# Grouped-head attention beside a GELU MLP, float32: the MLP's first bank in a pool of its own, `hh` products ahead of `hl` in one block, and a different order and shape of the first loads

## The chip, the cores and the metric

The kernel runs on one core of a Trainium2 chip. The metric is the device time of one execution in microseconds. PE is TensorE (its weight load is PEld), DVE is VectorE, ACT is ScalarE, POOL is GpSimd, and SP is SyncE, which here only issues DMAs.

## The reference

x has 2048 tokens of 448 features. Two branches read the same normalised tokens and are added to x.

```python
def _A_ref(x, wq, wk, wv, wo):        # 16 heads of 28, one key and value head for all
    q = (x @ wq).reshape(B, S, H, Dh).transpose(0, 2, 1, 3)
    k, v = x @ wk, x @ wv
    p = _softmax(jnp.einsum("bhqd,bkd->bhqk", q, k) * Dh ** -0.5)
    o = jnp.einsum("bhqk,bkd->bhqd", p, v)
    return o.transpose(0, 2, 1, 3).reshape(B, S, H * Dh) @ wo

def _B_ref(x, w1, b1, w2, b2):
    y = _layernorm(x)
    h = _gelu(jnp.einsum("bsd,df->bsf", y, w1) + b1)   # 1792 wide
    return jnp.einsum("bsf,fd->bsd", h, w2) + b2

xn = _layernorm(x)
return x + _A_ref(xn, wq, wk, wv, wo) + _B_ref(xn, w1, b1, w2, b2)
```

## The kernel before, in words

Tokens are cut into 16 tiles of 128, and these into 4 chunks of 512. Products that need full precision are made of rounded parts: a high part (`xh`, `wah`, `w1h`, `w2h`, `hh`) and the rest (`xl`, `wal`, `w1l`, `w2l`, `hl`), and a product is high times high, high times low and low times high, added up in a PSUM bank. The order on each engine is that of the code (`manual_schedule`); the pools and semaphores decide only what an instruction waits for.

There are three stages.

1. **Projections** (`norm_first`, then the loop over chunks with `q_slot`). For a tile, DVE takes the statistics (`bn`, line 208), `bn_end` makes the mean and the reciprocal deviation out of them (ACT's square root at line 193, then DVE's lines 196 to 199 and the shift at line 242), `center` normalises on ACT (line 284) and writes a doubled last part on DVE or POOL (line 288), and `turn` transposes on PE (line 299), copies the high part out on ACT (line 300) and the low part on DVE (line 303). `norm_first` does that for chunk 0 in two halves of two tiles, with idle products (`spin`, line 432) on PE between. `q_slot` makes 128 columns of q, k, v for a chunk in a bank `qp`; its `evac` copies the bank out on ACT (line 393) and DVE (lines 392 and 400), and SP stores the parts to DRAM (`qd`) and into `ks`. In the meantime `w1_split` and `split_a` cut the weights into parts on ACT and POOL.
2. **MLP** (`mlp1`, `mlp2`). For a chunk c and each of 14 slices ft of 128 hidden units, `mlp1` makes the first layer in a bank of the ring `s0` to `s3` (`spare`, 11 products), and ACT, DVE and POOL make the GELU and its parts `hh` and `hl` of it. `mlp2` follows two slices later and adds 12 products to four banks `m2`, one for each token tile. In the first chunk `w2_split` cuts w2 on ACT (line 376) and DVE (line 377) between them.
3. **Attention** with scores, exponentials on ACT, weighted sums of v, and the output product.

PSUM has 8 banks. In the projections the pools `qpp` (4 banks) and `mp` (3 banks) hold seven of them. When they close (`ph1a.close()`), the pool of the ring `ra` (4 banks) and that of `m2` (4 banks) are laid over them, and the first product into a bank waits until its former content has been read. In the same way the tiles `w2h` and `w2l` lie in SBUF where the tiles of the projections lay, `qe` among them, which SP's stores read; ACT's first `w2h` therefore waits for all eight DMA lanes.

A lane is one of eight semaphores that DMAs take in turn, those of SP's and of ACT's queue together. A DMA that gets a lane whose former DMA has not landed waits for it at its issue, and all behind it on that queue wait too. The loads at the start stand in this order: x's tiles 0, 1, and 2 and 3 together (SP), wv and wk (ACT), wq (SP), x's tiles 4 to 7, b1, b2 (`b2b`), tiles 8 to 11, then slices of w1 and the other tiles of x. `load_rows` loads the last 64 of the 448 rows of a weight twice, into both halves of the partitions, with a DMA for each. `b2b` is first read by POOL at line 636, in the 12th block of the MLP.

Of the kernel before, what the change touches and what calls it, by code (L numbers as in the profile page):

```python
# [10 lines left out]
F32 = mybir.dt.float32  # L11
# [5 lines left out]
PSUM = bass.MemoryType.PSUM  # L17

P = 128
S, D, H, DH, F = 2048, 448, 16, 28, 1792  # L20
NT = S // P
CT = 4
# [17 lines left out]
def block_kernel(ctx, tc, x, wq, wk, wv, wo, w1, b1, w2, b2, out):  # L40
    nc = tc.nc
    pe, act, dve, pool = nc.tensor, nc.scalar, nc.vector, nc.gpsimd
# [3 lines left out]
        return t.bitcast(F32)  # L46

    keep = ctx.enter_context(tc.tile_pool(name="keep", bufs=1))
    dram = ctx.enter_context(tc.tile_pool(name="dram", bufs=1, space=bass.MemoryType.DRAM))
    xt_p = ctx.enter_context(tc.tile_pool(name="xt", bufs=len(KEPT)))  # L50
    xl_p = ctx.enter_context(tc.tile_pool(name="xl", bufs=len(KEPT)))
# [23 lines left out]
    b2b = wp.tile([P, D], F32, name="b2b")  # L75
# [17 lines left out]

    def load_rows(dst, src, cols, q=nc.sync):
        q.dma_start(dst[:, 0:3, :], src[0:384, cols].rearrange("(b p) n -> p b n", p=P))
        q.dma_start(dst[0:64, 3, :], src[384:448, cols])
        q.dma_start(dst[64:128, 3, :], src[384:448, cols])

    def load_x(t0, n):
        if t0 < 2 * CT:  # L100
            c, k = divmod(t0, CT)
            dst = first_raws[c][:, k:k + n, :]
            nc.sync.dma_start(dst, xv[:, t0:t0 + n, :])
            return
        for t in range(t0, t0 + n):
            nc.sync.dma_start(xin[t], xv[:, t, :])
# [11 lines left out]
    wal = wqp.tile([P, 3, CW], F32R, name="wal")  # L118
    kvraw = wqp.tile([P, 4, 2, DH], F32, name="kvraw")
    load_rows(kvraw[:, :, 0, :], wv, slice(0, DH), nc.scalar)  # L120
    load_rows(kvraw[:, :, 1, :], wk, slice(0, DH), nc.scalar)
    def pair():
        return wqp.tile([P, 4, D], F32, name="pair", bufs=1)

    qraw = pair()
    load_rows(qraw, wq, slice(0, D))
    load_x(CT, CT)
    make_identity(nc, ident)
# [10 lines left out]
    pool.memset(f(qm), 0.0)  # L139
    b1r = wqp.tile([NF, P], F32, name="b1r", bufs=1)  # L140
    nc.sync.dma_start(b1r, b1.rearrange("(a p) -> a p", p=P))
    nc.sync.dma_start(b2b, b2[None, :].to_broadcast([P, D]))
    load_x(2 * CT, CT)

    def split_a(src, at):
# [58 lines left out]
    def bn(t):  # L204
        c = t // CT
        if t % CT == 0:
            sts[c] = tmp.tile([P, CT, 6], F32, name="st", bufs=2)
        dve.bn_stats(sts[c][:, t % CT, :], xin[t])

    def bn_end(c, k0=0, n=CT):  # L210
        for k in range(k0, k0 + n):
            dve.bn_aggr(lnp[:, CT * c + k, :], sts[c][:, k, :])
        ts = slice(CT * c + k0, CT * c + k0 + n)
        norms = (False, True) if c else (False,)
        r = rstd(lnrq[:, 0:len(norms), ts], lnp[:, ts, 1], n, norms)
        at = next(r)
        yield
        next(r)
        shift(c in KEPT, ts)
        yield  # L220
        if c in KEPT:
            ratio = ratios[c] = tmp.tile([P, CT], F32, name="ratio", bufs=3)
            dve.tensor_mul(ratio, at[:, 1], lnq[:, ts])
            dve.tensor_mul(ratio, ratio, lnr[:, ts])
        elif c:
            shift(True, ts)
        yield
# [41 lines left out]
    def norm_parts(c, second, first=False, bank=mtile):  # L269
        again, second = second, second or c in KEPT  # L270
        xh = xt_p.tile([P, 4, CW], F32R, name="xh")
        xl = xl_p.tile([P, 4, CW], F32R, name="xl")
        xts[c, second and c not in KEPT] = xh, xl
        xns = {}

        def center(k):
            t = CT * c + k
            if first:
                xn = f(wqp.tile([P, 2, CW], F32R, name="qe", bufs=5))[:, 0, :]
            else:  # L280
                xn = (wqp if k % 2 and not again else tmp).tile([P, 4 * P], F32, name="xn", bufs=1)
            scale, bias = (lnq, lnqb) if second else (lnr, lnb)
            src = lines.pop(t) if again else xin[t]
            act.activation(xn[:, 0:D], src, AF.Identity, bias=bias[:, t:t + 1], scale=scale[:, t:t + 1])
            xns[k] = xn

            def doubled():
                (pool if 0 < c else dve).tensor_scalar(
                    xn[:, D:512], src[:, 384:448], scale[:, t:t + 1], bias[:, t:t + 1], op0=ALU.mult, op1=ALU.add)

            if first and k == 1:
                return doubled
            doubled()

        def turn(k, lows=None):
            sl = slice(k * P, (k + 1) * P)
            pt = bank([P, 4, P])
            for b in range(4):
                pe.transpose(pt[:, b, :], xns[k][:, b * P:(b + 1) * P], ident)
            act.activation(xh[:, :, sl], pt, AF.Copy)  # L300

            def low():
                dve.tensor_sub(xl[:, :, sl], pt, f(xh[:, :, sl]))

            low() if lows is None else lows.append(low)

        return center, turn

    def norm_first(bank):
        center, turn = norm_parts(0, False, True, bank)  # L310
        ends = [bn_end(0, 0, 2), bn_end(0, 2, 2)]
        lows = []
        bn(0)
        bn(1)
        next(ends[0])
        next(ends[0])
        center(0)
        bn(2)
        bn(3)
        doubled = center(1)  # L320
        next(ends[1])
        doubled()
        next(ends[1])
        spin(16)
        turn(0, lows)
        spin(3)
        turn(1, lows)
        center(2)
        center(3)
        for low in lows:  # L330
            low()
        spin(6)
        turn(2)
        spin(1)
        turn(3)
        next(first)
# [13 lines left out]
    def w1_load(s):  # L350
        raw = rawtile([P, 4, HD])
        load_rows(raw, w1, slice(s * HD, (s + 1) * HD))
        wl_q.append(raw)

    def w1_load2(s):
        raw = pair()
        load_rows(raw, w1, slice(s * HD, (s + 2) * HD))
        wl_q.extend((raw[:, :, 0:HD], raw[:, :, HD:D]))
# [64 lines left out]
    load_x(3 * CT, CT)  # L423
    w1_load(1)
    w1_load2(2)

    def qbank(shape):
        return qpp.tile(shape, F32, name="qp")

    def spin(n, t=None):  # L430
        for _ in range(n):
            pe.matmul(idle if t is None else t, ident, ident, start=True, stop=True)

    idle = mtile([P, P])
    norm_first(qbank)
    g = stats(1)
    later_one = lambda g=g: next(g)
# [29 lines left out]
    for c in range(NCH):  # L467
        if c + 1 < NCH:
            center, turn = norm_parts(c + 1, False, bank=lambda shape: (qbank, mtile)[next(turns) % 2](shape))
        for i in range(4):  # L470
# [24 lines left out]
            if i in ((1, 3), (1, 2), (1, 3), (0, 2))[c]:  # L495
                n = 2 * c + (i - 1 if c == 1 else i // 2 if c == 3 else i // 3)
# [57 lines left out]
    ring_a = ctx.enter_context(tc.tile_pool(name="ra", bufs=1, space=PSUM))  # L554

    turn_a = itertools.count()

    def spare(shape=(P, CW)):
        return ring_a.tile(list(shape), F32, name=f"s{next(turn_a) % 4}")

    ph1b = ExitStack()
    hp = ph1b.enter_context(tc.tile_pool(name="hp", bufs=3))
# [24 lines left out]
    def mlp2(c, ft, then=None):  # L587
        if ft == 0:
            m2s[c] = [m2p.tile([P, CW], F32, name=f"m2_{k}")[:, 0:D] for k in range(CT)]
        m2 = m2s[c]  # L590
        hh, hl = hs.pop((c, ft))
        terms = ((hh, w2h), (hh, w2l), (hl, w2h))
        for k in range(CT):
            for i, (h, w) in enumerate(terms):
                pe.matmul(m2[k], h[:, k * P:(k + 1) * P], w[:, ft, :], start=(ft == 0 and i == 0),  # L595
                          stop=(ft == NF - 1 and i == 2))
            if ft == NF - 1:
                t = CT * MLP_ORDER[c] + k
                a = lines.pop(t)
                dve.tensor_add(a, a, m2[k])  # L600
                nc.sync.dma_start(ad[:, t, :], a)
            if then is not None:
                then()

    early = []
# [4 lines left out]
    def score_bank():  # L610
        n = next(turn_s) % 7 if ring_b else 0
        return ring_b[0].tile([P, CW], F32, name=f"t{n - 4}") if n > 3 else spare()
# [10 lines left out]
    for c in range(len(KEPT), NCH):  # L623
        g = norm_gen(MLP_ORDER[c], spare)
        for i in range(2 * CT + 1):
            norms[NF * (c - 1) + 4 + i] = lambda g=g: next(g, None)
    for n in range(len(mslots) + 2):
        c, ft = mslots[n] if n < len(mslots) else (NCH, n - len(mslots))
        if 3 <= ft < 11 and ft % 2 and len(KEPT) <= c + 1 < NCH:
            line(CT * MLP_ORDER[c + 1] + (ft - 3) // 2)  # L630
        k = ft - (10 if c < NCH - 1 else 5)
# [21 lines left out]
        if n >= len(mslots):  # L653
            t = f(xl_p.tile([P, 4, CW], F32R, name="xl"))
            early.extend(t[:, k, :] for k in range(4))
            mlp2(*mslots[n - 2], then=lambda: scores(*todo.pop(0)))
        elif n >= 2:
            mlp2(*mslots[n - 2])
# [216 lines left out]
```

## Time and profile before

| | us |
|---|---|
| median of 3 runs (899.61 to 900.98) | 900.62 |
| the profiled execution's own time | 901.05 |
| its span | 899.2 |
| PE busy in it | 883.6 |

A row of the timeline gives the start in us from the span's start, the duration, the engine, the line, what is written and read, and in brackets the idle time ahead of it with what ended it. Where instructions of one kind follow each other, they are merged into a row with their count. A row of waits gives the waiting engine and line, what it waited for, the sum, the number and the longest. The stages are easy to find in the timeline: the first transpose on PE is at 8.04 us, the first MLP product at 66.08 us, and the last second-layer product ends at 353 us.

### The profile page before, as it was taken

What the parts mean: (1) busy time and instruction counts of PE and PEld (TensorE: products, weight loads), DVE (VectorE), ACT (ScalarE), POOL (GpSimd) and SP (SyncE); (2) the same over time, 40 slices, a digit from 0 to 9 for tenths busy, and PEclk for the clock granted to TensorE, in tenths of its full rate; (3) what the DMA queues carried; (4) which work ended last, traced back from release to release, by engine and by line L of the source; (5) the groups of instructions that cost most, each with busy time, mean ns of one, the idle gap of its engine ahead of it and who ended that gap; (6) DMA issues with size and microseconds to landing.
All of it is one profiled execution on the core that took longest, in us unless ns stands there. A gap on an engine that the chain in (4) does not pass through costs nothing.

```text
span 899.2 us, 13110 instructions
## 1 busy us (share of the span) xinstructions
PE 883.6 (98%) x4925; PEld 572.8 (64%) x4925; DVE 313.3 (35%) x584; ACT 670.8 (75%) x1285; POOL 156.4 (17%) x149
## 2 busy tenths in 40 slices
PE   8989999999999999999999999999999999999996
PEld 7867888888888887444554554554555555555552
DVE  7865445344445343222132132132132132232223
ACT  5764444333444346999999999999999999999993
POOL 6443343233235342000000000000000000000000
PEclk9999999999999999999999999999999999999999
DMA  9692112002001402412013021013031113031001
GB/s 294 197 277 68 42 62 82 1 0 83 11 24 41 90 11 78 104 41 52 13 41 93 11 83 52 20 33 93 11 86 49 30 28 89 12 93 42 1 1 44
DMA packets 35022, 55.86 MB, mean 62 GB/s; under 512 B 5694, under 2 KB 21644, under 8 KB 34956
## 3 DMA queue, kind: packets, MB, share of 16 engines
q1 hardware_dynamic: 33548, 54.42, 21.6%
q8 instruction: 40, 0.66, 0.3%
q10 hardware_dynamic: 1408, 0.57, 0.2%
q14 instruction: 26, 0.21, 0.1%
HBM read 39.23 MB, written 14.68 MB: 60 GB/s over the span
## 4 chain that ended last, share of the span: by engine, by line
PE 91%; DVE 3%; ACT 2%; DMA 2%; issue 1%; SPq 0%; POOL 0%; ACTq 0%; DVEq 0%; POOLq 0%
PE po L727 26%; PE s L616 17%; PE m L595 14%; PE t L616 12%; PE s L175 12%; PE s L180 1%; PE s L178 1%; PE qp L175 1%; PE s L694 1%; PE s L695 1%; PE s L696 1%; DMA qd<-qe 1%; PE t L694 1%; PE t L695 1%; PE t L696 1%
## 5 line engine op out<-in xcount | busy, mean ns | idle before, releaser
L618 ACT ACTIVATE p<-s 128x512 f32<-128x512 f32 x582 | 316.9, 679 | 16.1 <-PE s L616 16.0
L618 ACT ACTIVATE p<-t 128x512 f32<-128x512 f32 x434 | 243.9, 680 | 11.0 <-PE t L616 11.0
L727 PE MATMUL po<-p,vs 128*32 128x512 f32 x2032 | 237.7, 597 | 0.0
L616 PE MATMUL s<-xh,ks 128*128 128x512 f32 x590 | 180.3, 406 | 0.0
L616 PEld LDWEIGHTS s<-xh,ks 128*128 128x128 f32 x590 | 107.6, 188 | 65.3 <-ACT p L618 23.4
L616 PE MATMUL t<-xh,ks 128*128 128x512 f32 x434 | 136.9, 406 | 0.0
L727 PEld LDWEIGHTS po<-p,vs 128*32 128x32 f32 x2032 | 56.3, 109 | 123.9 <-issue 118.5
L576 ACT ACTIVATE hx<-s,b1t 128x512 f32<-128x512 f32 x56 | 38.5, 687 | 115.4 <-PE s L180 105.7
L616 PEld LDWEIGHTS t<-xh,ks 128*128 128x128 f32 x434 | 79.3, 188 | 49.0 <-ACT p L618 18.3
L584 POOL TENSOR_TENSOR hl<-hx,hh 128x512 fp32r<-128x512 f32 x56 | 77.6, 1386 | 184.8 <-DVE hh L583 175.7
L718 POOL TENSOR_TENSOR otl<-oc,oth 128x512 fp32r<-128x512 f32 x15 | 19.4, 1295 | 488.7 <-DVE oth L717 450.8
L595 PE MATMUL m<-w2l,hh 128*128 128x448 f32 x224 | 82.6, 369 | 0.9 <-DVE w2l L377 0.9
L595 PE MATMUL m<-w2h,hh 128*128 128x448 f32 x224 | 82.4, 368 | 0.5 <-DVE a L600 0.4
L595 PE MATMUL m<-w2h,hl 128*128 128x448 f32 x224 | 82.0, 366 | 0.7 <-POOL hl L584 0.7
L578 DVE SCALAR_TENSOR_TENSOR hz<-hz,hx 128x512 f32<-128x512 f32 x56 | 45.4, 811 | 106.1 <-ACT hz L577 106.0
L579 ACT ACTIVATE hz<-hz 128x512 f32<-128x512 f32 x56 | 35.4, 632 | 49.9 <-DVE hz L578 49.9
L175 PE MATMUL s<-xh,w1h 128*128 128x512 f32 x168 | 66.4, 395 | 2.4 <-DVE qe L400 2.4
L698 DVE TENSOR_TENSOR row<-row,s 128x448 f32<-128x448 f32 x33 | 20.5, 622 | 133.6 <-PE s L696 133.6
L175 PE MATMUL s<-xl,w1h 128*128 128x512 f32 x168 | 66.4, 395 | 0.0
L175 PE MATMUL s<-xh,w1l 128*128 128x512 f32 x168 | 66.2, 394 | 0.0
L698 DVE TENSOR_TENSOR row<-row,t 128x448 f32<-128x448 f32 x27 | 16.8, 622 | 115.3 <-PE t L696 115.3
L580 DVE SCALAR_TENSOR_TENSOR hx<-hz,hx 128x512 f32<-128x512 f32 x56 | 39.1, 699 | 43.3 <-ACT hz L579 43.3
(174 smaller groups left out, 925.2 us busy)
## 6 DMA issues: line engine op xcount, KB each, us to landing
xh<-qd SPq DMA_DIRECT2D x64, 224.0 KB
qd<-qe SPq DMA_DIRECT2D x24, 256.0 KB
a<-in_A_x_dram SPq DMA_DIRECT2D x24, 224.0 KB
ad<-a SPq DMA_DIRECT2D x16, 224.0 KB
qm<-qd SPq DMA_DIRECT2D x64, 56.0 KB
row<-ad SPq DMA_DIRECT2D x16, 224.0 KB
raw<-in_B_w_dram SPq DMA_DIRECT2D x7, 448.0 KB
out_dram<-row SPq DMA_DIRECT2D x14, 224.0 KB
```

Of the source, the lines that this page charges most:

```text
L175: pe.matmul(ps, w, v, start=(n == 0), stop=False)
L576: act.activation(hx, ph, AF.Identity, bias=b1t[:, ft:ft + 1])
L578: dve.scalar_tensor_tensor(hz, hz, 1.0, hx, op0=ALU.add, op1=ALU.mult)
L579: act.activation(hz, hz, AF.Tanh, scale=GELU[1])
L580: dve.scalar_tensor_tensor(hx, hz, 1.0, hx, op0=ALU.add, op1=ALU.mult)
L584: pool.tensor_sub(hl, hx, f(hh))
L595: pe.matmul(m2[k], h[:, k * P:(k + 1) * P], w[:, ft, :], start=(ft == 0 and i == 0), stop=(ft == NF - 1 and i == 2))
L616: pe.matmul(s, ks[:, kt * P:(kt + 1) * P], qss[u][:, j, :], start=True, stop=True)
L618: act.activation(p, s, AF.Exp, scale=SCALE)
L698: dve.tensor_add(a, a, po)
L718: pool.tensor_sub(otl, oc, f(oth))
L727: pe.matmul(pos[u][32 * j:32 * j + 32, :], vs[:, kt, :], ps[u, kt, j], start=(kt == 0), stop=(kt == NT - 1))
```

## The change

1. A pool `r0` with one bank is opened at the very start, and `s0` of the ring comes from it; `s1` to `s3` stay in `ra`, which has three banks now.
2. In the very first block of the second layer (c = 0, ft = 0), the `hh` products of all four token tiles come first, then those of `hl`.
3. `load_rows` loads the doubled last rows with one DMA that reads its source twice.
4. `b2b` is loaded after the first slices of w1 instead of ahead of x's tiles 8 to 11.
5. In `norm_first`, `bn(2)` comes between the two steps of `bn_end` for tiles 0 and 1, ahead of the reciprocal.

```diff
     keep = ctx.enter_context(tc.tile_pool(name="keep", bufs=1))
+    ring_0 = ctx.enter_context(tc.tile_pool(name="r0", bufs=1, space=PSUM))
...
     def load_rows(dst, src, cols, q=nc.sync):
         q.dma_start(dst[:, 0:3, :], src[0:384, cols].rearrange("(b p) n -> p b n", p=P))
-        q.dma_start(dst[0:64, 3, :], src[384:448, cols])
-        q.dma_start(dst[64:128, 3, :], src[384:448, cols])
+        load_last(dst, src, cols, q)
+
+    def load_last(dst, src, cols, q=nc.sync):
+        q.dma_start(dst[:, 3, :], src[384:448, cols][None].to_broadcast([2, 64, dst.shape[-1]]))
...
     nc.sync.dma_start(b1r, b1.rearrange("(a p) -> a p", p=P))
-    nc.sync.dma_start(b2b, b2[None, :].to_broadcast([P, D]))
     load_x(2 * CT, CT)
...
         next(ends[0])
+        bn(2)
         next(ends[0])
         center(0)
-        bn(2)
         bn(3)
         doubled = center(1)
...
     w1_load2(2)
+    nc.sync.dma_start(b2b, b2[None, :].to_broadcast([P, D]))
...
     def spare(shape=(P, CW)):
-        return ring_a.tile(list(shape), F32, name=f"s{next(turn_a) % 4}")
+        n = next(turn_a) % 4
+        return (ring_a if n else ring_0).tile(list(shape), F32, name=f"s{n}")
...
         terms = ((hh, w2h), (hh, w2l), (hl, w2h))
+        early = c == 0 and ft == 0
+        if early:
+            for k in range(CT):
+                for i, (h, w) in enumerate(terms[:2]):
+                    pe.matmul(m2[k], h[:, k * P:(k + 1) * P], w[:, ft, :], start=(i == 0), stop=False)
         for k in range(CT):
             for i, (h, w) in enumerate(terms):
+                if early and i < 2:
+                    continue
```

Three places in the order of the instructions. The first is on DVE, in `norm_first`: `st` holds a tile's statistics, `rs` the terms of the reciprocal deviation, `lnrq` and `lnb` its scale and shift, `qe` the centred tile. Before:

```order
L208 BN_STATS st<-rows 128x6 x2
L212 BN_AGGR lnp<-st 128x2 x2
L194 TENSOR_SCALAR rs_193<-lnp 128x2
L196 RECIPROCAL rs_193<-rs_193 128x2
L197 SCALAR_TENSOR_TENSOR rs_193<-rs_193 128x2
L198 TENSOR_TENSOR rs_193<-rs_193 128x2
L199 SCALAR_TENSOR_TENSOR lnrq<-rs_193 128x2
L242 SCALAR_TENSOR_TENSOR lnb<-lnp,lnrq 128x2
L288 TENSOR_SCALAR qe<-rows,lnrq,lnb 128x64
L208 BN_STATS st<-rows 128x6 x2
```

The same place of the changed kernel:

```order
L210 BN_STATS st<-rows 128x6 x2
L214 BN_AGGR lnp<-st 128x2 x2
L196 TENSOR_SCALAR rs_190<-lnp 128x2
L210 BN_STATS st<-rows 128x6
L198 RECIPROCAL rs_190<-rs_190 128x2
L199 SCALAR_TENSOR_TENSOR rs_190<-rs_190 128x2
L200 TENSOR_TENSOR rs_190<-rs_190 128x2
L201 SCALAR_TENSOR_TENSOR lnrq<-rs_190 128x2
L244 SCALAR_TENSOR_TENSOR lnb<-lnp,lnrq 128x2
L290 TENSOR_SCALAR qe<-rows,lnrq,lnb 128x64
L210 BN_STATS st<-rows 128x6
```

The third tile's statistics have moved ahead of the reciprocal of the first two tiles.

The second place is on PE, where the MLP begins: `qp` is the last bank of the projections, `s_...` a bank of the ring, and the brackets hold the semaphores for which an instruction waits. Before:

```order
L178 MATMUL qp<-xh,wah 128x512
L180 MATMUL qp<-xl,wah 128x512
L175 MATMUL s_926<-xh,w1h 128x512 [waits DVE_49,PE_49]
L175 MATMUL s_926<-xl,w1h 128x512
L175 MATMUL s_926<-xh,w1l 128x512
```

The same place of the changed kernel, with the end of the first bank and the start of the second:

```order
L180 MATMUL qp<-xh,wah 128x512
L182 MATMUL qp<-xl,wah 128x512
L177 MATMUL s_920<-xh,w1h 128x512
...
L182 MATMUL s_920<-xl,w1h 128x512
L177 MATMUL s_947<-xh,w1h 128x512 [waits DVE_49,PE_49]
```

The wait for the projections' banks has moved from the first bank of the ring to the second, 11 products later.

The third place is on PE, in the first block of the second layer: `m_0` to `m_3` are the four banks. Before:

```order
L595 MATMUL m_0_999<-w2l,hh 128x448 [waits DVE_49]
L595 MATMUL m_0_999<-w2h,hl 128x448 [waits Pool_49]
L595 MATMUL m_1_1000<-w2h,hh 128x448
L595 MATMUL m_1_1000<-w2l,hh 128x448
L595 MATMUL m_1_1000<-w2h,hl 128x448
```

The same place of the changed kernel:

```order
L601 MATMUL m_0_993<-w2l,hh 128x448 [waits DVE_49]
L601 MATMUL m_1_994<-w2h,hh 128x448
L601 MATMUL m_1_994<-w2l,hh 128x448
L601 MATMUL m_2_995<-w2h,hh 128x448
L601 MATMUL m_2_995<-w2l,hh 128x448
L601 MATMUL m_3_996<-w2h,hh 128x448
L601 MATMUL m_3_996<-w2l,hh 128x448
L606 MATMUL m_0_993<-w2h,hl 128x448 [waits Pool_49]
L606 MATMUL m_1_994<-w2h,hl 128x448
```

The wait for POOL's `hl` stood at the third product of the block and stands at the ninth now; that for DVE's `w2l` is at the second, as it was.

## The prediction

> **What bounds the kernel now.** I read the page's busy times first, then the list of waits with PE as the waiting engine.
>
> ```profile
> PE 883.6 (98%) x4925; PEld 572.8 (64%) x4925; DVE 313.3 (35%) x584; ACT 670.8 (75%) x1285; POOL 156.4 (17%) x149
> ```
>
> ```profile
> PE s L175 <- DVE qe L400: 2.4, 1, 2.4
> PE qp L299 <- ACT qe L284: 1.3, 1, 1.3
> PE m L595 <- DVE w2l L377: 0.9, 2, 0.7
> ```
>
> TensorE (PE) works 98% of the span, so a microsecond counts only where PE waits or runs slowly. The longest wait is a single one of 2.4 us, at the MLP's first product (line 175, tile `s`), until DVE has finished line 400. The diff bears on all three. PE's timeline around the first, and the same stretch cut into windows (PE, PEld, DVE, ACT, POOL busy; granted clock, DMA share, GB/s):
>
> ```profile
> 63.25 0.39 PE L180 MATMUL qp<-xl,wah 128*128 128x512 f32 x1
> 66.08 0.77 PE L175 MATMUL s<-xh,w1h 128*128 128x512 f32 x1 [2.44 <-DVE qe L400]
> ...
> 70.24 0.39 PE L175 MATMUL s<-xh,w1h 128*128 128x512 f32 x1
> ...
> 72.75 0.39 PE L175 MATMUL s<-xh,w1h 128*128 128x512 f32 x1
> ```
>
> ```profile
> 63.00:66.05 3.05, 0.64 (x3) 0.19 (x2) 2.82 (x5) 1.63 (x3) 2.27 (x2) 1.00 0.87 263
> 66.05:69.50 3.45, 3.42 (x8) 2.80 (x9) 0.00 (x0) 0.00 (x0) 0.00 (x0) 0.51 0.89 320
> 69.50:72.00 2.50, 2.50 (x12) 2.05 (x12) 0.26 (x1) 1.27 (x2) 0.00 (x0) 1.00 0.03 10
> ```
>
> The wait costs more than its own length. After it the clock is granted at 0.51 for about 3.4 us, in which PE gets through 8 products. The first group of 11 takes 70.24 - 66.08 = 4.16 us, the second 72.75 - 70.24 = 2.51 us: another 1.65 us is lost to the clock.
>
> **The first bank.** Bank `s0` now has a pool of its own, and PE's order shows its first product without a wait; the wait for DVE stands at the second bank's first product. The projections' last product starts at 63.25 and the pace is 2.51/11 = 0.23 us, so the first group runs from 63.48 to 65.99. The second bank is released when the first was, at 66.08. So the second group starts at 66.08 where it started at 70.24: **-4.16 us** (2.51 of it the gap, 1.65 the clock). What is left at the second bank is 0.1 us of waiting; each further 0.1 us by which the release slips costs 0.1 us. The first group's other inputs were split and in use long before.
>
> The Trainium skill, "TensorE: Matmul & The Clock Gate", in its part on the HAM clock gate, says that PE falls to half rate after at least one idle window of about 3.4 us, in windows that run freely. By that rule a 2.44 us gap would not slow the clock, and the first term would be 2.51 us instead of 4.16 us. The window rows differ from it: half clock follows this gap at once.
>
> **The order of the first second-layer products.** ACT, DVE, POOL and PE there, each from its own timeline:
>
> ```profile
> 73.01 0.94 ACT L376 ACTIVATE w2h<-raw 128x896 fp32r<-128x896 f32 x1
> ```
>
> ```profile
> 73.86 0.43 DVE L583 CAST hh<-hx 128x512 fp32r<-128x512 f32 x1
> 74.26 1.09 DVE L377 SCALAR_TENSOR_TENSOR w2l<-raw,w2h 128x896 fp32r<-128x896 f32 x1
> ```
>
> ```profile
> 74.43 2.05 POOL L584 TENSOR_TENSOR hl<-hx,hh 128x512 fp32r<-128x512 f32 x1 [8.57 <-DVE hh L583]
> ```
>
> ```profile
> 75.24 0.36 PE L595 MATMUL m<-w2h,hh 128*128 128x448 f32 x1
> 76.54 0.47 PE L595 MATMUL m<-w2h,hl 128*128 128x448 f32 x1 [0.67 <-POOL hl L584]
> ...
> 78.67 0.39 PE L175 MATMUL s<-xh,w1h 128*128 128x512 f32 x1
> ...
> 81.19 0.36 PE L595 MATMUL m<-w2h,hh 128*128 128x448 f32 x1
> ...
> 83.63 0.39 PE L175 MATMUL s<-xh,w1h 128*128 128x512 f32 x1
> ```
>
> The first block of 12 takes 78.67 - 75.24 = 3.43 us, the next 83.63 - 81.19 = 2.44 us: 0.99 us is lost, most of it waiting for POOL's `hl`. With eight `hh` products ahead (8 x 0.2 = 1.6 us), `hl` is asked for 7.0 us after the second group's start, and POOL had it after 76.48 - 70.24 = 6.24 us, so that wait goes. What is late next is `w2l`, in the second product. ACT's `w2h` ran 2.77 us after the second group's start (73.01 - 70.24), but it waits for every DMA lane, because its tile lies in memory that the projections' stores still read:
>
> ```profile
> 62.27 4.92 SPq L409 DMA_DIRECT2D qd<-qe  x8
> ```
>
> SP issues the last stores until 67.19, and the windows show the transfers busy (0.89) until 69.5, then 0.03. Before, that was over in time. Now 69.5 is 3.4 us after the second group's start: `w2h` runs 0.65 us later in the chain, and `w2l` ends at 3.4 + 0.94 + 1.09 = 5.4 us, where PE wants it at 5.2 us (75.24 - 70.24 + 0.2); with the handovers I take 0.4 us of waiting. So the block loses 0.4 instead of 1.0 us: **-0.6 us**. Bounds: -1.0 us (stores drain sooner, as SP has fewer issues behind it) and 0 (the drain ends 0.6 us later). The other `w2l` wait, at the third block, hangs on a chain that moves along with PE; I leave it at nothing. In blocks after the first the sequence is as before.
>
> **The start.** DVE, ACT, PE and POOL, from the timeline of the first 30 us:
>
> ```profile
> 3.78 0.63 DVE L208 BATCH_NORM_STATS2 st<-rows 128x6 f32<-128x448 f32 x1 [3.78 <-DMA rows<-in_A_x_dram]
> 4.50 1.28 ACT L420 ACT_TABLE_LOAD   x1 [4.50 <-DMA kvraw<-in_A_wv_dram]
> 4.60 0.63 DVE L208 BATCH_NORM_STATS2 st<-rows 128x6 f32<-128x448 f32 x1 [0.19 <-DMA rows<-in_A_x_dram]
> 5.47 0.17 DVE L194 TENSOR_SCALAR rs<-lnp 128x2 f32<-128x2 f32 x1
> 5.91 0.28 ACT L193 ACTIVATE rs<-lnp,one 128x2 f32<-128x2 f32 x1
> 6.22 0.17 DVE L196 RECIPROCAL rs<-rs 128x2 f32<-128x2 f32 x1 [0.57 <-ACT rs L193]
> 7.22 1.41 ACT L284 ACTIVATE qe<-rows,lnb,lnrq 128x448 f32<-128x448 f32 x2 [1.04 <-DVE lnb L242]
> 7.46 1.14 DVE L208 BATCH_NORM_STATS2 st<-rows 128x6 f32<-128x448 f32 x2
> 8.04 0.66 PE L299 MATMUL qp<-ident,qe 128*128 128x128 f32 x4 [1.27 <-ACT qe L284]
> 10.54 0.41 POOL L158 TENSOR_SCALAR wah<-pair 128x256 fp32r<-128x256 f32 x1 [0.61 <-DMA pair<-in_A_wq_dram]
> 11.71 0.32 POOL L160 TENSOR_TENSOR wah<-pair,wah 64x64 fp32r<-64x64 f32 x1
> 11.85 0.60 PE L299 MATMUL qp<-ident,qe 128*128 128x128 f32 x4
> 17.18 0.19 PEld L178 LDWEIGHTS qp<-xh,wah 128*128 128x128 f32 x1 [0.21 <-POOL wah L153]
> ```
>
> PE runs nearly without a gap from 8.04 to 63.64, so what sets 8.04 moves all that follows: reciprocal, scale and shift, ACT line 284, first transpose. The reciprocal waited for ACT until 6.22, and ACT was late (table load at 4.50) because its last key/value load had waited for a DMA lane. The change merges loads, so ACT is free sooner. But `bn(2)` now stands ahead of the reciprocal on DVE, and it needs the third load of x (tokens' tiles 2 and 3, 448 KB). The first two, 224 KB each, had landed by 3.78 and 4.60, 0.82 us apart; at that rate 448 KB land 1.64 us later, at 6.24. Then bn(2) takes half of 1.14 us, and the reciprocal starts at about 6.83 instead of 6.22: **+0.61 us**. Queued behind it on DVE are that whole chain and, through ACT, PE's transposes; PE's idle stretch there grows from 1.27 to 1.9 us. Bounds: if the load is in by 5.64 (5.47 + 0.17), bn(2) runs beside ACT's square root and costs nothing; a gain is excluded because bn(2) alone reaches 6.2. At the other end the load had landed by 7.46, since DVE ran bn(2) then without a wait: reciprocal at 8.06, +1.84 us. I take 6.24, the value of the nearest rows.
>
> SP's own waits show what held wq's load (line 95) at its issue:
>
> ```profile
> SPq L95 <- DMA rows<-in_A_x_dram: 1.6, 1, 1.6
> ```
>
> Now it has a lane at once. It lands no later than before, and POOL's splits finish no later, while PE comes 0.61 us later: the 0.21 us wait at 17.18 goes, **-0.21 us**. More cannot be had: ahead of the first projection PE's transposes end last (11.85 + 0.60 = 12.45), after POOL's first split (11.71 + 0.32 = 12.03).
>
> **Cost nothing.** The merged 64-row loads move the same bytes; they take seven issues off SP and two off ACT's queue, and none of PE's waits names a store or a later load. Moving `b2b` on SP past fourteen loads (x's tiles 8 to 15 and the first slices of w1) takes its 224 KB out of their way; POOL first reads it some ten MLP blocks of 5 us (2.51 + 2.44) after 66 us, so its landing is covered many times over. SP's first `ks` stores now have four issues fewer ahead of them. Should a merged load land late, DVE's or POOL's splits would be late by as much, and PE has the 0.6 us by which it comes later itself as cover.
>
> **The sum.** The profiled execution took 901.05 us, its span 899.2. 901.05 - 4.16 - 0.60 + 0.61 - 0.21 = 896.7 us. It stands 0.43 us above the median of the runs (900.62) and beyond the highest (900.98); I take off half of that: **896.5 us**.
>
> **Rivals.**
> - *The slow clock appears elsewhere.* PE's idle stretch at the start grows to 1.9 us, on the way to the 2.44 us that was followed by half clock; 1.27 us was not. Then 1.65 us come back: 896.5 + 1.65 = 898.2. Chance 0.12.
> - *The slow stretch was not the gap's.* If it comes by its own timing and stays, the first term is 2.51 us: 898.2. The windows speak against it (0.51 exactly from the gap's end). It is the result by the Trainium skill's clock-gate rule above, which the trace does not bear out. Chance 0.10.
> - *The third load lands at 7.46.* Reciprocal 1.23 us later than I take it: 897.7. Chance 0.09.
> - *The change does not do what it says*, and the first group still waits out the last evacuation. Only the other terms are left: 900.8 - 0.2 = 900.6. PE's order speaks against it. Chance 0.04.
> - *Slower.* wq's 672 KB, issued 1.6 us sooner, share the transfer engines with the third load of x, and bn(2) holds the whole chain. Place: DVE ahead of the reciprocal. If the load lands only with wq, near 10.4 (POOL saw wq at 10.54), the reciprocal starts at 11.0, 4.8 us late; PE idles long enough for slow clock, +1.65. 901.05 - 4.76 - 0.21 + 4.8 + 1.65 = 902.5. It decides from a landing at about 8.9 on. Against it: wq is issued behind that load on the same queue. The Trainium skill, "DMA: Bandwidth & Descriptors", under queues, rings and completion order, states that each DMA engine consumes the descriptors of one queue in order; by it this rival falls away. No run here shows yet how these two loads share. Chance 0.03.
>
> **How the numbers follow.** The forecast as worked has the other 0.62. Its own ends: 896.5 - 0.61 - 0.4 = 895.5 with the late costs at nothing, less the other half of the offset, 895.2; upward 897.7 with the late load. Both clock rivals (898.2) have to be inside, with 0.6 for the first block's bound: 895.2 to 898.8. Faster by over 0.2% means under 898.8, about what a measurement of this kernel tells from no change: the forecast and the first three rivals, 0.93, less 0.04 for two of them at once: 0.89; same 0.08; slower 0.03.
>
> **What would show it.** Right: no idle of PE ahead of the first `s` product, granted clock 1.00 through that stretch, under 0.3 us ahead of the second bank; the `hl` wait gone, some 0.4 us before the first `w2l` product; DVE's reciprocal at 6.8 with bn(2) waiting for the rows ahead of it. The prediction is wrong if bn(2) does not wait, if half clock stands anywhere between 5 and 890 us, or if the release of the second bank comes over 0.5 us after the first group's end.

## The result: 913.76 us, slower by a ratio of 1.0149 [1.0136, 1.0162]

Four runs of the changed kernel took 913.07 to 914.86 us, four of the kernel before beside them 899.61 to 901.12 (median 900.80). The profiled execution took 913.07 us and its span 911.3 us, 12.1 us more than before. All of it lies in the first 91 us. Start of the same instruction on PE, from the two timelines:

| PE's instruction | before | after | later by |
|---|---|---|---|
| first transpose | 8.04 | 9.88 | 1.84 |
| first q product | 12.21 | 17.04 | 4.83 |
| chunk 1, first transposes | 20.74 | 27.19 | 6.45 |
| chunk 2, second transposes | 34.96 | 41.43 | 6.47 |
| chunk 3, first transposes | 44.30 | 52.49 | 8.19 |
| last projection product | 63.25 | 72.63 | 9.38 |
| second bank of the ring | 70.24 | 76.86 | 6.62 |
| first second-layer product | 75.24 | 85.99 | 10.75 |
| MLP product behind that block | 78.67 | 90.88 | 12.21 |
| last group of products | 891.61 | 903.73 | 12.12 |

One step goes the right way: between the last projection product and the second bank 2.76 us are won. All others lose. The page's first part and the list of waits, PE as the waiting engine, after:

```profile
PE 886.2 (97%) x4925; PEld 574.6 (63%) x4925; DVE 313.1 (34%) x584; ACT 670.9 (74%) x1285; POOL 155.4 (17%) x149
```

```profile
PE m L601 <- ACT w2h L378: 3.9, 1, 3.9
PE qp L301 <- ACT qe L286: 3.0, 1, 3.0
PE qp L177 <- POOL wah L160: 2.7, 1, 2.7
...
PE qp L301 <- ACT xn L286: 1.7, 1, 1.7
...
PE s L177 <- DVE qe L402: 1.4, 1, 1.4
```

PE does the same 4925 products; new waits stand ahead of it. The same places in PE's timeline:

```profile
9.88 0.66 PE L301 MATMUL qp<-ident,qe 128*128 128x128 f32 x4 [2.97 <-ACT qe L286]
...
17.04 0.39 PE L177 MATMUL qp<-xh,wah 128*128 128x256 f32 x1 [2.75 <-POOL wah L160]
...
72.85 0.39 PE L177 MATMUL s<-xh,w1h 128*128 128x512 f32 x1
...
76.86 0.47 PE L177 MATMUL s<-xh,w1h 128*128 128x512 f32 x1 [1.35 <-DVE qe L402]
...
85.99 0.47 PE L601 MATMUL m<-w2h,hh 128*128 128x448 f32 x1 [3.87 <-ACT w2h L378]
```

The first `s` product (72.85) has no wait any more, as its own bank should give. The engines named in the other brackets waited themselves. DVE, POOL and ACT, each from its own timeline, and the chain of waits (start, length, what was under way):

```profile
7.56 0.63 DVE L210 BATCH_NORM_STATS2 st<-rows 128x6 f32<-128x448 f32 x1 [2.11 <-DMA rows<-in_A_x_dram]
```

```profile
15.45 0.28 POOL L160 TENSOR_SCALAR wah<-kvraw 128x112 fp32r<-128x112 f32 x1 [8.17 <-DMA kvraw<-in_A_wk_dram]
```

```profile
49.55 0.60 ACT L395 ACTIVATE qe<-qp 128x512 fp32r<-128x512 f32 x1 [3.08 <-DMA qd<-qe]
...
84.98 0.95 ACT L378 ACTIVATE w2h<-raw 128x896 fp32r<-128x896 f32 x1 [6.45 <-DMA qd<-qe]
```

```profile
4.63 12.30 DMA rows<-in_A_x_dram
23.60 12.82 DMA pair<-in_B_w_dram
47.55 6.68 DMA qd<-qe
56.55 10.31 DMA pair<-in_B_w_dram
81.27 3.46 DMA qd<-qe
```

These waits end at transfers: x's third load, wk, the stores of q. In the chain stand loads of 10 to 13 us. So the question is why transfers that move no more bytes are late. The windows while POOL waits for wk (the last two numbers are the DMA share and GB/s), after and then before:

```profile
13.00:14.00 1.00, 1.00 (x9) 1.00 (x10) 0.41 (x1) 0.91 (x2) 0.00 (x0) 1.00 0.34 112
14.00:15.00 1.00, 0.29 (x3) 0.06 (x1) 0.70 (x2) 0.94 (x3) 0.00 (x0) 1.00 0.12 49
15.00:16.00 1.00, 0.00 (x0) 0.00 (x0) 0.65 (x1) 0.66 (x1) 0.47 (x2) 1.00 0.14 57
...
18.50:22.00 3.50, 3.50 (x18) 3.40 (x17) 3.40 (x11) 0.76 (x3) 3.50 (x5) 0.51 0.92 281
```

```profile
13.00:14.00 1.00, 1.00 (x9) 0.80 (x8) 1.00 (x3) 0.82 (x2) 1.00 (x2) 1.00 1.05 400
14.00:15.00 1.00, 1.00 (x9) 1.00 (x10) 1.00 (x3) 0.00 (x0) 1.00 (x2) 1.00 1.07 383
15.00:16.00 1.00, 1.00 (x7) 0.87 (x7) 1.00 (x5) 0.00 (x0) 1.00 (x2) 1.00 1.09 300
```

The transfer engines are not crowded, they are nearly idle: from 14 to 16 us a share of 0.12 to 0.14 of 16 engines, which is that of two engines (2/16 = 0.125), moving 49 to 57 GB/s where 300 to 400 were moved before. A mean share could also be sixteen engines at an eighth of their time. The trace's records of single packets exclude that: from 15 to 16 us two packets are under way for 97% of the time and three for the rest, each of 7168 bytes in 0.275 us; before, 15 to 21 are under way from 13 to 16 us. By an estimate from these rates, wq's doubled part, 2 x 112 KB, takes some 4.3 us at 53 GB/s. SP could not use the others, as its own timeline and waits show:

```profile
6.48 9.14 SPq L109 DMA_DIRECT2D a<-in_A_x_dram  x4
...
62.48 4.88 SPq L411 DMA_DIRECT2D qd<-qe  x2
```

```profile
SPq L109 <- DMA kvraw<-in_A_wk_dram: 7.6, 2, 5.0
...
SPq L411 <- DMA pair<-in_B_w_dram: 4.1, 2, 3.9
```

It stood for 9.14 us at four loads of x, 7.6 us of it because its lanes were held by loads of wk (two waits), and later for 4.88 us at two stores behind w1's loads (`pair`). So the theory is: **a load whose source is read twice, with the count of 2 outermost, is spread over two transfer engines only; it holds its lane for that long, and SP's queue and PE wait behind it.** The Trainium skill, "DMA: Bandwidth & Descriptors", under "Why a DMA increments its semaphore by 16 and not by 1", states that the engine count is the largest k up to 16 that divides both access patterns' slowest dimension; under "Rules for kernel authors" it names a leading zero-stride broadcast of c copies as confined to at most c engines. Here c is 2, and the share of 0.12 to 0.14 and the two packets under way agree.

Rivals: fewer DMAs shift the lanes' turns, and something waits for the wrong lane; bn(2) delays the chain; b2b's place; the half clock (0.51 from 18.5 us on) does it.

### The profile page after: what moved, and what is told of

Read it like the earlier page. It is cut to its first block, busy times and chain, and to the rows that moved or that the text cites. A ratio compares the mean times of both kernels' runs of the same rounds, so it can differ in the third digit from the quotient of the medians.

```text
span 911.3 us, 13100 instructions
## 1 busy us (share of the span) xinstructions
PE 886.2 (97%) x4925; PEld 574.6 (63%) x4925; DVE 313.1 (34%) x584; ACT 670.9 (74%) x1285; POOL 155.4 (17%) x149
## 4 chain that ended last, share of the span: by engine, by line
PE 88%; DMA 6%; DVE 3%; ACT 1%; SPq 1%; issue 1%; ACTq 0%; DVEq 0%
PE po L738 26%; PE s L627 16%; PE m L606 14%; PE t L627 12%; PE s L177 11%; DMA pair<-in_B_w_dram 3%; DMA qd<-qe 2%; DMA rows<-in_A_x_dram 1%; PE s L182 1%; PE s L180 1%; PE s L705 1%; PE s L706 1%; PE s L707 1%; PE t L705 1%; PE t L706 1%; PE t L707 1%
```

## The experiments

Each stands as a median of its runs, and as a ratio to the kernel before on the same chip. "Outside" is the time of a run less its span.

| | median us | ratio, 95% | spans | outside |
|---|---|---|---|---|
| e1: change, two loads | 900.66 | 0.9995 [0.9984, 1.0006] | 895.1-896.1 | 1.8-2.0 (3), 4.6-5.4 (7) |
| e2: merged loads only | 911.38 | 1.0118 [1.0101, 1.0135] | 909.1-910.4 | 1.8 |
| e3: change, 128 rows | 897.55 | 0.9974 [0.9961, 0.9988] | 895.6-898.3 | 1.8 |
| e4: change, bn(2) back | 912.56 | 1.0128 [1.0110, 1.0145] | 909.1-911.7 | 1.8-1.9 |
| e5: e1, bn(2) back | 899.84 | 0.9989 [0.9979, 0.9999] | 894.8-897.0 | 1.8-2.0 (3), 4.6-5.8 (9) |
| e6: bank only | 897.65 | 0.9974 [0.9965, 0.9983] | 894.9-898.3 | 1.8-1.9 |
| e7: bn(2) only | 901.20 | 1.0006 [0.9996, 1.0015] | 897.8-900.0 | 1.8-1.9 |
| e8: merged w1 only | 909.70 | 1.0100 [1.0086, 1.0115] | 904.5-906.7 | 4.8-5.2 |
| e9: merged wq, wk, wv only | 907.09 | 1.0073 [1.0058, 1.0088] | 904.2-905.7 | 1.8-1.9 |
| e10: bank and early block | 897.16 | 0.9967 [0.9954, 0.9980] | 895.0-895.6 | 1.8-1.9 |
| e11: b2b's place only | 901.25 | 1.0016 [1.0006, 1.0027] | 897.1-898.8 | 1.8-1.9 (6), 4.6-5.5 (6) |
| e12: e1, b2b back | 897.74 | 0.9968 [0.9956, 0.9980] | 895.4-897.1 | 1.8-1.9 |

**e1, the change with two loads.**

```diff
     def load_last(dst, src, cols, q=nc.sync):
-        q.dma_start(dst[:, 3, :], src[384:448, cols][None].to_broadcast([2, 64, dst.shape[-1]]))
+        q.dma_start(dst[0:64, 3, :], src[384:448, cols])
+        q.dma_start(dst[64:128, 3, :], src[384:448, cols])
```

> The changed kernel, with the last 64 weight rows loaded by two DMAs again. Theory (the merged load runs on few DMA engines and holds up all that shares them): POOL no longer waits 8 us for wk, the third load of x lands near 6.2 us, the first projection product starts by 13.5 us instead of 17.0, and the time is 897 us (895 to 899). Rival one (the statistics moved ahead of the reciprocal are the main cost): the first transpose stays at 9.9 us and the time stays above 905 us.

The span falls from 911.3 to 895.1 us, under that of before. PE's timeline at the MLP's second bank and first second-layer block, and DVE's at bn(2):

```profile
71.22 0.37 PE L602 MATMUL m<-w2h,hh 128*128 128x448 f32 x1
72.50 0.47 PE L602 MATMUL m<-w2l,hh 128*128 128x448 f32 x1 [0.91 <-DVE w2l L380]
...
74.03 0.97 PE L607 MATMUL m<-w2h,hl 128*128 128x448 f32 x4
74.84 0.39 PE L178 MATMUL s<-xh,w1h 128*128 128x512 f32 x1
```

```profile
5.86 0.63 DVE L211 BATCH_NORM_STATS2 st<-rows 128x6 f32<-128x448 f32 x1 [0.33 <-DMA rows<-in_A_x_dram]
6.40 0.15 DVE L199 RECIPROCAL rs<-rs 128x2 f32<-128x2 f32 x1
```

The waits at transfers are gone with the merged loads: POOL's first wk part runs at 8.69 us (8.87 before, 15.45 after). That the median is still 900.66 comes from outside the span, which e11 and e12 take up.

**e2, the merged loads alone** in the kernel before (the line that e1 removes, and nothing else of the change).

> The kernel before, with the merged load of the last 64 weight rows as its only change. Theory: POOL waits for wk until about 15 us, the first projection product comes about 4 us late, the w2h of the MLP waits for stores, 910 to 917 us. Rival one (statistics ahead of the reciprocal): no difference from the kernel before, 900.8 us.

10.6 us are lost by this edit alone. The list of waits, PE as the waiting engine:

```profile
PE qp L174 <- POOL wah L157: 3.6, 1, 3.6
PE s L174 <- DVE qe L399: 3.6, 1, 3.6
PE qp L298 <- ACT xn L283: 2.1, 1, 2.1
```

**e3, one load of 128 different rows**: as many DMAs and bytes as in the changed kernel, with 128 outermost. The last block of each weight then holds other rows than the reference's.

```diff
-        q.dma_start(dst[:, 3, :], src[384:448, cols][None].to_broadcast([2, 64, dst.shape[-1]]))
+        q.dma_start(dst[:, 3, :], src[320:448, cols])
```

> The changed kernel, but the merged load reads 128 different rows (320 to 447) instead of 64 rows twice, so the products use other weights in the last block and the output is another one; bytes, number of DMAs and lanes are those of the changed kernel, and only the outermost dimension of the source is 128 instead of 2. Theory (2 engines of 16 carry the doubled read): as with two loads, 897 us (895 to 899). Rival two (it is the number of DMAs, their order on the lanes, or one wait for all 128 rows): stays at 911 to 915 us.

With one DMA in place of two, and the lanes turning as in the changed kernel (wq issued at 2.24 us in both), it is faster than before. So neither the number of DMAs nor their lanes cost the time; the form of the source does. The run changes two things in it, the outermost count and the double reading of rows. A packet of 7168 bytes takes 0.272 us here at 8 to 10 us and 0.275 us in the changed kernel, so what differs is how many are under way and not how fast each is; that speaks for the count. The same doubled load with the 64 rows outermost would be the closest test; it wasn't tried.

**e4, the change with bn(2) behind the reciprocal again**, which tells whether bn(2) is the cause.

```diff
         next(ends[0])
-        bn(2)
         next(ends[0])
         center(0)
+        bn(2)
         bn(3)
```

> The changed kernel with the third tile's statistics back behind the reciprocal. Theory: the first transpose is at 8.0 us or earlier again, but POOL still waits for wk until 15 us, so the first product stays near 17 us and the time at 911 to 914 us. Rival one: 899 us or less.

It keeps nearly all of the loss (912.56; the interval overlaps that of the change). The first transpose is at 7.59 us again, as expected, but the first q product starts at 15.23 us and not near 17. PE waits 4.1 us for `w2h`, 3.2 us for `wah` and 2.7 us for `xn`. Beside e2 it shows a second thing: with merged loads, the bank of its own, the new order and b2b's place together show no gain (912.56 against 911.38). e2 waits 3.6 us in front of the first bank, e4 has that wait no more and stands 4.1 us in front of `w2h` instead.

**e5, e1 with bn(2) back** (both diffs above).

> The changed kernel with two loads for the last weight rows and with the third tile's statistics behind the reciprocal again: bank, order of the first block and place of b2b are left of the change. The span should be 895 us, 4 us under that of the kernel before (bank: -4.1; first block: 0 to +0.2; statistics: 0.2 less than in the run with two loads). Time: 897 us if the time around the span is 1.9 us as in the kernel before; 900 to 901 us if it is 5 us as in most runs with two loads.

Its median span is 895.1 us against 895.9 us of e1: by these two, bn(2)'s new place costs 0.8 us. The span is the expected one; nine of the twelve runs end 4.6 to 5.8 us after it, which makes the median 899.84.

**e6, the first bank alone** (the two hunks on `ring_0` in the kernel before).

> The kernel before with the bank in a pool of its own as its only change. Theory of the prediction's first term: the second bank's first product at 66.1 instead of 70.24 us, granted clock 1.00 there, span 895 us, -4.1 us; the first block of the second layer waits for w2l and hl some 1.0 to 1.4 us, since w2h now meets the end of the stores. Rival (the slow clock comes by its own timing): -2.5 us, span 896.7 us.

Faster than both kernels. PE and POOL, each from its timeline:

```profile
66.05 0.47 PE L176 MATMUL s<-xh,w1h 128*128 128x512 f32 x1
...
71.14 0.37 PE L597 MATMUL m<-w2h,hh 128*128 128x448 f32 x1
72.41 0.47 PE L597 MATMUL m<-w2l,hh 128*128 128x448 f32 x1 [0.91 <-DVE w2l L378]
72.72 0.36 PE L597 MATMUL m<-w2h,hl 128*128 128x448 f32 x1
```

```profile
70.12 1.29 POOL L586 TENSOR_TENSOR hl<-hx,hh 128x512 fp32r<-128x512 f32 x1 [4.24 <-DVE hh L585]
```

POOL has `hl` at 71.41, a microsecond before the product that reads it: the wait for `w2l` now covers the one for `hl`, without any new order.

**e7, bn(2) alone** (that hunk in the kernel before).

> The kernel before with the third tile's statistics ahead of the reciprocal as its only change. By the run with two loads the third load is in at 5.9 us and the reciprocal starts 0.2 us late: +0.2 us, 901 us, no difference that can be told. By the prediction's term it would be +0.6 us. Rival (the move itself holds the start up by 1.8 us, as the trace of the changed kernel reads at first): 902.6 us.

Not told apart from before. Its profile holds something else, the same gap as before and no half clock behind it; PE's timeline and two windows with the gap in them (the third number from the end is the granted clock; the last section says why they are cut there):

```profile
66.73 0.47 PE L175 MATMUL s<-xh,w1h 128*128 128x512 f32 x1 [2.44 <-DVE qe L400]
```

```profile
62.44:65.85 3.41, 1.85 (x9) 1.16 (x7) 2.63 (x5) 2.62 (x4) 1.61 (x1) 1.00 0.81 241
65.85:69.26 3.41, 2.53 (x11) 2.13 (x12) 0.73 (x2) 0.01 (x1) 0.66 (x1) 1.00 1.02 372
```

**e8 and e9, the merged load in the kernel before for w1 alone, and for wq, wk and wv alone** (e9 has `is not`).

```diff
         q.dma_start(dst[:, 0:3, :], src[0:384, cols].rearrange("(b p) n -> p b n", p=P))
+        if src is w1:
+            q.dma_start(dst[:, 3, :], src[384:448, cols][None].to_broadcast([2, 64, dst.shape[-1]]))
+            return
```

> The kernel before, with the merged load for the slices of w1 alone (six loads); wq, wk and wv keep their two. The first projection product should be at 12.2 us as before, with no wait for wk, but the later stretch (x's chunk 3 on ACT, the last evacuations, w2h) late by what the changed kernel lost after its first product: 905 to 908 us. If the loads at the start are what counts, it is 901 us.

> Before, with the merged (doubled-source) load for wq, wk and wv only; w1's slices keep two loads. Theory (such a load runs on few DMA engines): POOL's key part comes as late as in the kernel with all loads merged, so the first q product starts near 15.8 us instead of 12.2 (+3.6), the long stall brings a stretch of half clock (+1.7), and PE's waits for xn and qe in the projections (48 us) and at the MLP's start stay as in the kernel before: 903.5 to 906. If w1's loads are nearly all of the loss instead, and the late start is caught up later: within 1.5 us of before. If wv, wk and wq cost as much as all merged loads together (the stores' delay comes from them): 909 to 912.

Each alone makes the median span 6 to 7 us longer (904.8 and 905.2, against 898.7 and 898.3 of the kernel before beside them), and both together (e2) 10.6: they overlap in part. e8's time of 909.70 us lies above the 905 to 908 expected, because all four of its runs end some 5 us after the span and not 1.8. e8 waits in the projections and at the MLP's start, where the stores queue behind w1's loads; e9 waits at the start. PE's waits of e8, then PE's timeline of e9 with its windows:

```profile
PE s L178 <- DVE qe L403: 3.5, 1, 3.5
PE qp L302 <- ACT xn L287: 3.3, 1, 3.3
```

```profile
15.88 0.58 PE L178 MATMUL qp<-xh,wah 128*128 128x256 f32 x1 [3.67 <-POOL wah L161]
```

```profile
14.00:15.00 1.00, 0.00 (x0) 0.00 (x0) 0.00 (x0) 0.58 (x1) 0.63 (x2) 1.00 0.12 50
16.00:22.00 6.00, 6.00 (x25) 5.63 (x26) 5.23 (x14) 1.25 (x4) 5.73 (x8) 0.50 0.78 246
72.40:73.40 1.00, 0.98 (x4) 0.85 (x5) 0.00 (x0) 0.00 (x0) 0.00 (x0) 1.00 1.03 371
73.40:77.00 3.60, 3.60 (x10) 2.81 (x9) 0.00 (x0) 0.42 (x1) 0.00 (x0) 0.53 0.40 138
```

e9 shows the two engines again (0.12, 50 GB/s). It lost 6.9 us, over a microsecond more than the upper end of what was expected: the stall of 3.67 us came as foreseen, but half clock behind it lasted all of 16 to 22 us and cost, by an estimate (half of 6 us), about 3 us, not 1.7.

**e10, the bank and the early block** in the kernel before (the hunks on `ring_0` and `early`).

> Before, with the first bank in its own pool and the hh products first in the first second-layer block; loads and bn(2) as before. Theory: the early block is worth little, since its wait moves to w2l: within 0.5 us of the bank alone (897.65), so 897.2 to 898.2, and the end of the program outside the span stays at 1.8 us. Rival A (the recorded term): 897.0 from -0.6. Rival B: the early block is what made the two kernels with two loads slow outside the span: 900 to 901 with the same span near 895.

```profile
71.25 0.36 PE L599 MATMUL m<-w2h,hh 128*128 128x448 f32 x1
72.52 0.47 PE L599 MATMUL m<-w2l,hh 128*128 128x448 f32 x1 [0.91 <-DVE w2l L378]
...
74.85 0.39 PE L176 MATMUL s<-xh,w1h 128*128 128x512 f32 x1
```

The block takes 74.85 - 71.25 = 3.60 us; e6's, in the old order, 3.61 us. Its median is the lowest of all, but its interval overlaps that of e6. No gain of the new order is shown; the two ratios differ by 0.0007, so the times alone don't exclude 0.6 us either.

**e11 and e12, b2b's place**: its move alone in the kernel before (that hunk), and e1 with the load back at its old place.

> Before, with only the load of b2b moved behind w1's first slices. Theory: costs and gains nothing in the span: 900.2 to 900.9. Rival: that move is what makes the program end later outside its span (4.6 to 5.8 us instead of 1.8): 903 to 904 with the span unchanged at 897.6 to 899.7.

> The change with the 64-row loads as two DMAs again and b2b loaded at its old place: the first bank, the early block and bn(2) are left of it. Theory (the place of b2b's load is what makes many executions end 3 us later outside the span, when no load is merged): spans of 895.1 to 896.2 as with b2b moved, time outside the span 1.8 us in every run, 897.0 to 898.0. Rival (the combination of the other edits does it): the median stays at 900 to 901, with 4.6 us and more outside the span in most runs.

e11's expectation was a mixture of both cases: six of twelve runs end 4.6 to 5.5 us after the span, six 1.8 to 1.9. e12 took the move away and all six of its runs end at 1.8 to 1.9. So among the kernels with two loads of the last rows it goes with b2b's place: 22 of 34 runs with the move (e1, e5, e11) end late, none of 31 without it (e6, e7, e10, e12). What happens there stays open. It isn't the move alone: e8 ends late in all of its four runs without it, and the changed kernel, e3 and e4 never do with it.

## Why the prediction was wrong

**The step that failed** is the first sentence of "Cost nothing": the merged 64-row loads move the same bytes. They do, but over two engines instead of sixteen (two packets under way instead of 15 to 21). That step looked at bytes and issues and not at how the transfer is spread. It cost 10.6 us alone (e2), and its cover, "the 0.6 us by which it comes later itself", was short of a landing 6.6 us late (wk at 15.45 instead of 8.87). That wq "lands no later than before" falls with it: in e9, which merges the same three loads, ACT waits for it until 14.42 us (POOL had it by 10.54 before). The same loads then held the lanes of SP's stores, so `w2h` ran at 84.98 us, 8.1 us after the second group's start, where 3.4 us had been reckoned.

**The other steps**, measured without merged loads:

- *First bank, -4.16 us*: the mechanism and the place hold (second bank at 66.05 in e6, 66.08 forecast; no wait ahead of the first). The profile of e6 is 3.7 us shorter in span than that of before, but over ten runs the ratio is 0.9974 [0.9965, 0.9983], 1.5 to 3.2 us less time, not 4.16. Half clock stands behind this gap in the profiles of before, e9 and e11 and not in e7's, so the 1.65 us can be won in some executions only. The 71 runs of the kernel before that stand beside the experiments fall in two groups: spans of 897.2 to 898.0 us (25 runs) and of 898.3 to 900.0 us (46). That fits without showing it, as only one of such runs has a trace, the one with a span of 899.2 us from which the forecast was made. "Half clock follows this gap at once" was read from that one execution; the last section shows on what it depends.
- *Order of the first block, -0.60 us*: not shown (e10 against e6). The `hl` wait goes, as forecast, but by the bank already; what is late next is `w2l`, as forecast, by 0.91 instead of 0.4 us, since `w2h` ran 70.12 - 66.13 = 3.99 us after the second group's start in e10, not 3.4.
- *bn(2), +0.61 us*: in line with it, but not measured to tenths: e7 gives 0.5 us (-0.4 to 1.4), e1 less e5 0.8 us in the median span, while e12 and e10 hardly differ (0.9968 and 0.9967). x's third load, taken at 6.24 us, landed so that bn(2) ran at 5.86 to 6.66 us in e1, e3, e7 and e12; the reciprocal followed at 6.40 to 7.21 us (6.83 forecast, 6.22 before) and the first transpose at 8.20 to 8.99 (8.04 before). In the changed kernel bn(2) ran at 7.56, near the third rival's 7.46.
- *POOL's wait, -0.21 us*: gone in e1, where POOL's split ends at 16.50 us (17.13 before). That isn't by the mechanism forecast, since wq is issued at 3.67 us there, about as late as before (3.78).
- *b2b at nothing*: true in the span (e11), not outside it (about 3 us in half of e11's runs).

With two loads the span of e1's profile is 895.1 us; the terms made it 899.2 - 4.36 = 894.8. That they agree so well is luck in part: -0.60 and +0.61 cancel, and the former isn't there in the profiles. The MLP product behind the first block starts at 78.67 us before, at 74.75 with the bank alone (e6) and at 74.84 in e1, so the bank accounts for nearly all of it. The merged loads, costed at nothing, outweighed it.

**The rivals.** The slower one named a crowd on the transfer engines, at DVE, that decides at a landing of 8.9 us; the load landed at 7.56, and in e3, where wq is issued just as early (2.24 us, 3.78 before), at 6.37. So wq's earlier issue, its mechanism, is not what cost the time. The first rival, slow clock after a longer gap at the start, did happen (0.51 from 18.5 to 22 us, behind the 2.75 us wait for POOL) as a consequence of the late wk. With a second stretch from 86.8 to 90.3 us, behind the wait for `w2h`, it costs an estimated 3.4 of the 12.1 us (half of 2 x 3.41).

## What to carry to other kernels

Before two DMAs are merged into one with a repeated source, look at the outermost count of the pattern, not at the bytes: with 2 outermost the transfers ran at about 50 GB/s in a stretch where 300 to 400 were moved with two separate loads of 64 rows. Its mark here was a DMA share near 2/16 while an engine waited for a load. And a small load that is off the critical path is not free when it shares a lane and a queue with stores on which PE's next stage waits. Of this change, the bank of its own is worth keeping (e6, and e10 with the new order, 0.9967 [0.9954, 0.9980]).

## What was not expected of the hardware

- **Half clock depends on where a gap falls.** After the same gap of 2.44 us it set in at once (before), about a microsecond later (e9: 1.00 until 73.4, then 0.53) or not at all (e7). The clock records of the fourteen traces show why. In each of them, from the first stretch at full clock (it begins at 4.3 to 6.9 us) to the last fall near the end, every stretch of full or half clock lasts a whole multiple of 3.41 us, so the time is cut into windows of 3.41 us that start elsewhere in each execution. When PE stood idle for 2.0 us or more of a window at full clock, the next window had half clock (eleven windows, without those at the program's end); after 1.9 us or less it never had. In the kernel before, the window from 62.62 to 66.03 us holds nearly all of the gap, 2.39 us idle. In e7 a border at 65.85 cuts the gap into 1.56 and 0.88 us (3.41 - 1.85 and 3.41 - 2.53 in the rows shown there). The Trainium skill, "TensorE: Matmul & The Clock Gate", in its part on the HAM clock gate, says that the activity window runs freely, about 3.4 us long, and doesn't start with the work; the traces agree. Its condition of an idle window of about 3.4 us does not hold here: 2.0 us of idleness inside one window were enough.
- **Time outside the span** is 1.8 to 2.0 us in most runs and 4.6 to 5.8 us in others of the same kernel with the same span. In this kernel it hung on where one load of 224 KB stands in SP's program (e11, e12), and on which loads are merged (e8, e3, e4). The cause was not found.
